# Heads grouped by their place in the pair, and three small products run on eight or four tiles of the TensorE array

## The chip, the core and the metric

The program runs on one core of a Trainium2 chip. The metric is the device time of one execution in microseconds (us). The kernel before takes 1470.96 us, the median of three runs (1470.56 to 1471.3).

## What is computed

Eight batches (`B`), each of eight heads (`H`), 512 tokens (`S`), 32 states (`Ns`) and 64 elements (`D`): tokens read the states, states read the tokens, and what they read goes through two gated layers.

```python
def _attn_ref(x, state):
    scale = 1.0 / np.sqrt(D)
    scores = scale * np.matmul(x, state.transpose(0, 1, 3, 2))   # tokens x states
    a = softmax(scores)                                          # over the 32 states
    xread = np.matmul(a, state)
    scores2 = scale * np.matmul(state, x.transpose(0, 1, 3, 2))  # states x tokens
    a2 = softmax(scores2)                                        # over the 512 tokens
    sread = np.matmul(a2, x)
    return np.concatenate([xread, sread], axis=2)

x = attn_out  as  (B * (S + Ns)) x 512
x = ((x @ w_a) * (x @ w_b)) @ w_out        # 512 -> 1536 -> 512
h = x @ w_in                               # 512 -> 2048
return (h - np.tanh(h)) @ w_out2           # 2048 -> 512
```

## The kernel before

A block is one batch. Blocks 0 to 7 hold the 512 token rows of a batch; block 8 holds the state rows of all eight. The first layer of a block goes over `f` = 0 to 11, 128 hidden columns at a time. For each `f`, `AB` (L507) makes two products of 512 columns into a PSUM tile `pab` (12 matmuls each), multiplies them, and splits the result into a high and a low part (`ph`); `X1` (L533) multiplies that with the output weights into four accumulators `acc` (12 matmuls). The second layer (L679, and all from L897 on) follows when the first is through, and the change does not touch it.

**What is small.** The tokens' read is never formed: `xread @ w` is `a @ (state @ w)`, and `M` (L431) makes `state @ w` for one `f`, a tile `mx` of 128 rows (heads' states) by 512 columns. Blocks 0 and 1 take `mx` from `M` itself; for blocks 2 to 7 `M_later` (L470, tiles `mq` and `mst`) makes it during blocks 1 and 4, writes it to a DRAM tensor `md`, and `M_load` (L495) brings it back. The softmax work of the next block (class `Att`, L272) is spread over the twelve `f` of the block that runs (`stages`, L394): `scores` (`sc`), `scale`, softmax over states (`rows_max`, `rows_norm`, result `hl`) and over tokens (`cols_exp`, `cols_norm`), four transposes (`turn`, tile `pt`), and `sread` (`pr`), the states' read of the tokens.

**How the heads lie.** Two heads that are neighbours form a pair `p` (0 to 3): their elements fill the 128 partitions of `xT`, and their states stand beside each other in `stp`, whose 64 columns for a pair have zeros where a state would meet the other head. A group `G` before is two pairs, so `sc` is 128 rows: a matmul contracts over all 128 partitions and writes 64 of them. Everything from `scores` to `sevac` runs once for `G` = 0 and, some stages later, once for `G` = 1. These products have F32 operands, and each of their matmuls stands as two records in the trace; `AB` and `X1` have one record per matmul.

**What sets the order.** Each engine runs its instructions in the order that a scheduler gave them when the program was built. PSUM has eight banks: four are `acc`, two are `pab`, and all else of the first layer (`sc`, `pt`, `pr`, `mp`, `mq`, `pl`, `pa`) takes turns in two, `p0` and `p1` (`att`, L78). In block 0, `M` holds its bank through a round trip: ScalarE copies the high part out (L442), TensorE subtracts it (L443, weight `minus`), ScalarE copies the rest (L444). In block 1 the rest is VectorE's (L125). VectorE also decodes the weights, above all in block 0 (`words`, L117).

Of the kernel before, what the change touches and what calls it, by code (L numbers as in the profile page):

```python
# [8 lines left out]
F32 = mybir.dt.float32  # L9
# [7 lines left out]
KT = 4  # L17
# [27 lines left out]
def fused_kernel(ctx: ExitStack, tc, xT, xn, stp, stq, wA, wB, outT, outS):  # L45
# [23 lines left out]
    md = [[tc.dram_tile([nb, 2, 2, NST, 2, 256], F32, name=f"md{i}_{f}") for f in range(FA)]  # L69
# [202 lines left out]
    class Att:  # L272
# [12 lines left out]
        def load_xT(self, G, t=None):  # L285
            t = t or big.get([128, 2, 512], F32, "xTt", XIN)
            nc.sync.dma_start(t, xT[self.b, 2 * G : 2 * G + 2].rearrange("q p t -> p q t"))
            self.xT[G] = t

        def load_xn(self, G, t=None):  # L290
            t = t or big.get([128, 4, 256], F32, "xnt", XIN)
            nc.sync.dma_start(t, xn[self.b, :, 256 * G : 256 * G + 256].rearrange("(t p) c -> p t c", p=128))
            self.xn[G] = t

        def scores(self, G):
            ps = self.ps[G] = att.get([128, 512], F32, "sc")
            for q in range(2):
                p = 2 * G + q
                nc.tensor.matmul(ps[64 * q : 64 * q + 64, :], self.stp[:, 64 * p : 64 * p + 64],  # L299
                                 self.xT[G][:, q, :], start=True, stop=True)  # L300

        def scale(self, G, S=None):
            self.S[G] = S if S is not None else small.get([128, 512], F32, "S", AT)
            self.sm[G] = sp.tile([128, 36], F32, tag="sm", name="sm", bufs=2)
            nc.scalar.mul(self.S[G], self.ps[G], 0.125)
# [7 lines left out]
        def rows_max(self, G, L=None):  # L313
            L = self.L[G] = L if L is not None else small.get([128, 512], F32, "L", AT)
# [13 lines left out]
        def rows_norm(self, G):  # L328
# [11 lines left out]
            else:  # L340
                aT = small.get([128, 512], F32, "aT", AT)
                nc.vector.transpose(aT, L)
            hl = HL[self.b][G] = x_tile(2 * (self.b % 2 == 0) + G, [128, 2, 512], "hl")
# [19 lines left out]
        def turned(self, G, t=None):  # L363
            self.E2T[G] = t if t is not None else small.get([128, 4, 128], F32, "E2T", AT)
            nc.scalar.copy(flat(self.E2T[G]), self.pt[G])

        def sread(self, G):
            pr = self.pr[G] = att.get([128, 512], F32, "pr")
            for g in range(2):
                for t in range(4):  # L370
                    for q in range(2):
                        p = 2 * G + q
                        j = 2 * q + g
                        nc.tensor.matmul(pr[32 * p : 32 * p + 32, 64 * g : 64 * g + 64],  # L374
                                         self.E2T[G][:, t, 32 * j : 32 * j + 32],
                                         self.xn[G][:, t, 64 * j : 64 * j + 64],
                                         start=t == 0, stop=t == 3, skip_group_check=True)

        def sevac(self, G):
            if G == 0:  # L380
                self.SR = sp.tile([128, 128], F32, tag="SR", name="SR")
            r = slice(64 * G, 64 * G + 64)
            nc.scalar.copy(self.SR[r, :], self.pr[G][r, :128])
# [10 lines left out]
        def stages(self):  # L394

            none = lambda: None
            yield none, (lambda: (self.scores(0), self.load_xn(0)))
            yield (lambda: (self.scale(0), self.rows_max(0), self.cols_exp(0))), none
            yield (lambda: (self.cols_norm(0), self.rows_norm(0))), (lambda: self.turn(0))
            yield (lambda: self.turned(0)), (lambda: (self.sread(0), self.load_xT(1)))  # L400
            yield (lambda: self.sevac(0)), none
# [584 lines left out]
```

## Time and profile before

| | us |
|---|---|
| median of 3 runs | 1470.96 |
| lowest, highest | 1470.56, 1471.3 |
| the profiled execution's own time | 1472.2 |
| its span in the profile | 1470.4 |

By the page of the profile TensorE's matmuls (PE) are busy for 99% of the span, VectorE (DVE) 77%, ScalarE (ACT) 62%, GpSimd 11%. The chain of work that ended last is PE's for 96%: L424 (`pab` and `acc`) for 66%, and in the small products `mq` 3%, `mp` 2%, `pr` 1%, `sc` 1%. The ends of matmuls are modelled and they overlap, so what a group of them costs is read from the chain, which gives each piece the time until the next begins.

### The profile page before, as it was taken

Reading aid. Unit: us, or ns where it says so; the run is one execution under the profiler, and the core shown is the slowest. Engines: PE = TensorE matmul, PEld = TensorE weight load, DVE = VectorE, ACT = ScalarE, POOL = GpSimd, SP = SyncE. Lnnn points to the kernel's source line nnn. Section 1 sums busy time; section 2 is a strip of 40 time slices with the busy share of each in tenths; the row PEclk is TensorE's granted clock in tenths of the full one; section 3 lists DMA queues with packets and bytes.
Section 4 is the critical chain, followed back from the end, with each engine's and each line's share of the span. In section 5 each row is a group of like instructions: output and inputs, shape, how many; then the busy total and the mean of one; then the engine's idle time right before and its main releaser. Section 6 shows DMA issues by size and latency. Waiting matters only on the chain.

```text
span 1470.4 us, 23250 instructions
## 1 busy us (share of the span) xinstructions
PE 1451.6 (99%) x8660; PEld 1223.9 (83%) x8660; DVE 1128.3 (77%) x1969; ACT 904.4 (62%) x1721; POOL 167.6 (11%) x318
## 2 busy tenths in 40 slices
PE   6999999999999999999999999999999999999999
PEld 3776777777888777888988998998989889889998
DVE  6986546787543778773388899888989898898887
ACT  5764445565443556552367777767777776767675
POOL 0000000222000222220211111111001111111110
PEclk9999999999999999999999999999999999999999
DMA  8733435677455677753966656666675666656544
GB/s 292 242 131 109 153 129 179 216 230 230 123 136 149 188 235 233 237 186 115 314 204 190 207 179 207 194 197 208 187 222 172 209 200 190 209 171 214 169 146 127
DMA packets 102625, 280.44 MB, mean 191 GB/s; under 512 B 14064, under 2 KB 43248, under 8 KB 92784
## 3 DMA queue, kind: packets, MB, share of 16 engines
q0 software_dynamic: 40320, 178.28, 39.8%
q1 hardware_dynamic: 62192, 100.68, 20.7%
q8 instruction: 68, 1.11, 0.3%
q14 instruction: 45, 0.37, 0.1%
HBM read 216.53 MB, written 62.39 MB: 190 GB/s over the span
## 4 chain that ended last, share of the span: by engine, by line
PE 96%; DMA 1%; DVE 1%; ACT 1%; issue 0%; SPq 0%; ACTq 0%; DVEq 0%
PE acc L424 45%; PE pab L424 21%; PE px L609 12%; PE pz L609 6%; PE py L609 3%; PE mq L478 3%; PE mp L437 2%; PE pr L374 1%; PE sc L299 1%; DMA x1d<-ev 1%; DMA rawab<-in_wA 1%; PE pt L310 0%; PE mp L443 0%; PE pa L310 0%; DVE sm L324 0%
## 5 line engine op out<-in xcount | busy, mean ns | idle before, releaser
L424 PE MATMUL acc<-g,wo 128*128 128x512 f32 (+1 forms) x1728 | 436.7, 385 | 0.1
L424 PEld LDWEIGHTS acc<-g,wo 128*128 128x128 f32 x1728 | 293.7, 190 | 40.3 <-DVE g L649 0.3
L424 PE MATMUL acc<-ph,wo 128*128 128x512 f32 (+1 forms) x1296 | 305.1, 383 | 0.5 <-DVE sm L355 0.5
L424 PE MATMUL pab<-hl,mx 128*128 128x512 f32 x1152 | 293.6, 401 | 0.0
L424 PEld LDWEIGHTS acc<-ph,wo 128*128 128x128 f32 x1296 | 231.6, 188 | 52.6 <-issue 3.1
L424 PEld LDWEIGHTS pab<-hl,mx 128*128 128x128 f32 x1152 | 211.6, 189 | 61.8 <-issue 6.7
L524 DVE TENSOR_TENSOR ac<-ac,pab 128x512 f32<-128x512 f32 (+1 forms) x108 | 70.7, 654 | 144.4 <-PE pab L424 143.2
L256 POOL DMA_DIRECT2D wh<-whd x144 | 76.2, 529 | 674.6 <-PE pz L609 607.8
L644 ACT CAST g<-y 128x512 fp32r<-128x512 f32 (+1 forms) x144 | 86.0, 597 | 85.5 <-DVE y L640 84.4
L609 PEld LDWEIGHTS px<-T,wh 128*128 128x128 f32 x768 | 109.5, 190 | 11.0
L609 PE MATMUL px<-B,wh 128*128 128x256 f32 x768 | 113.6, 284 | 2.8 <-ACT snap L715 2.8
L633 DVE SCALAR_TENSOR_TENSOR y<-y,u 128x512 f32<-128x512 f32 (+1 forms) x144 | 95.0, 659 | 26.8 <-ACT y L625 26.1
L609 PEld LDWEIGHTS px<-B,wh 128*128 128x128 f32 x768 | 106.0, 192 | 8.8 <-ACT snap L715 3.3
L609 PE MATMUL pz<-T,wh 128*128 128x256 f32 x768 | 113.1, 283 | 0.0
L609 PE MATMUL px<-T,wh 128*128 128x256 f32 x768 | 112.8, 283 | 0.0
L521 ACT COPY ac<-pab 128x512 f32<-128x512 f32 (+1 forms) x108 | 60.5, 560 | 82.6 <-PE pab L424 82.5
L609 PEld LDWEIGHTS pz<-T,wh 128*128 128x128 f32 x768 | 105.9, 192 | 5.7
L640 DVE COPY_PREDICATED y<-k,t 128x512 f32<-128x512 int32 (+1 forms) x144 | 104.8, 728 | 2.7
L649 DVE TENSOR_TENSOR g<-y,g 128x512 fp32r<-128x512 f32 (+1 forms) x144 | 94.6, 657 | 9.3 <-ACT g L644 9.3
L634 DVE SCALAR_TENSOR_TENSOR u<-t,u 128x512 f32<-128x512 f32 (+1 forms) x144 | 94.3, 655 | 9.0 <-ACT k L629 1.0
L629 ACT ACTIVATE k<-u,consts 128x512 f32<-128x512 f32 (+1 forms) x144 | 99.8, 693 | 0.0
L625 ACT ACTIVATE y<-u,consts 128x512 f32<-128x512 f32 (+1 forms) x144 | 98.8, 686 | 0.7 <-DVE g L649 0.6
(234 smaller groups left out, 2056.8 us busy)
## 6 DMA issues: line engine op xcount, KB each, us to landing
wh<-whd POOLq DMA_DIRECT2D x64, 1024.0 KB, 5.3
wh<-whd POOLq DMA_DIRECT2D x72, 768.0 KB, 4.7
ml<-md POOLq DMA_DIRECT2D x72, 256.0 KB, 3.2
raw<-in_wB SPq DMA_DIRECT2D x32, 512.0 KB, 4.7
whd<-hlb POOLq DMA_DIRECT2D x64, 256.0 KB, 3.8
rawab<-in_wA SPq DMA_DIRECT2D x12, 1024.0 KB, 5.2
md<-mst SPq DMA_DIRECT2D x48, 256.0 KB, 2.6
x1d<-ev SPq DMA_DIRECT2D x32, 256.0 KB, 3.6
```

The lines of the kernel that those rows point to most:

```text
L256: nc.gpsimd.dma_start(t.rearrange("p a h c -> p a (h c)"), whd[j][:, a:b])
L424: nc.tensor.matmul(dst[:, cols], w[a], x[:, c, cols], start=first and i == 0, stop=last and i == 2)
L521: nc.scalar.copy(a[:, :n], pt[:, :n])
L524: at_v = nc.vector.tensor_tensor(a[:, :n], a[:, :n], pt[:, :n], ALU.mult)
L609: nc.tensor.matmul(dst, WP[s, piece][:, a, block(k)], XB[slots[s][0]][x][:, c, k, :], start=first and k == 0 and i == 0, stop=last and k = ...
L625: nc.scalar.activation(y, u, AF.Square, bias=consts[:, 0:1], scale=1.0)
L629: nc.scalar.activation(k, u, AF.Relu, bias=consts[:, 1:2], scale=1.0)
L633: nc.vector.scalar_tensor_tensor(y, y, PK, u, ALU.add, ALU.mult)
L634: nc.vector.scalar_tensor_tensor(u, t, C3, u, ALU.mult, ALU.mult)
L640: nc.vector.copy_predicated(y, k.bitcast(I32), t)
L644: nc.scalar.copy(GG[s, g][:, 0, : width(s)], EW[s, g][2])
L649: nc.vector.tensor_tensor(gt[:, 1, :n], EW.pop((s, g))[2], gt[:, 0, :n].bitcast(F32), ALU.subtract)
```

## The change

A group `G` is now the place in the pair: `G` = 0 has the first heads of all four pairs, `G` = 1 the second. A head's product contracts over its own 64 partitions alone and writes its own 32, so eight matmuls stand in for four, on eight tiles of the array (two by rows, four by columns). The two row halves write two PSUM tiles, in the two banks.

- `scores()` makes both groups at once; it needs both halves of `xT`, which are loaded together.
- `M` writes two tiles of 256 columns; each has its own copies and, in block 0, its own `minus` matmul.
- `sread()` makes both groups in one go, four column tiles of 32 rows at a time, with the same 32 matmuls in all as two visits had before. `sevac` is one copy in place of two.
- The second half of `xT` and of `xn` lies in a buffer that is later the block's `hl` of group 1.
- `md` has another layout, and `M_load` two transfers of 64 partitions for one of 128.
- `stages` has a new order; `rows_norm(1)` comes last.

```diff
+        def load_x(self, src, name, shape, places):
+            halves = []
+            for h in range(2):
+                t = places[h] if places else (big.get(shape, F32, name, XIN) if h == 0
+                                              else xp.tile(shape, F32, tag=f"x{self.hl(1)}", name=name))
+                nc.sync.dma_start(t, src(h))
+                halves.append(t)
+            return halves
-        def scores(self, G):
-            ps = self.ps[G] = att.get([128, 512], F32, "sc")
-            for q in range(2):
-                p = 2 * G + q
-                nc.tensor.matmul(ps[64 * q : 64 * q + 64, :], self.stp[:, 64 * p : 64 * p + 64],
-                                 self.xT[G][:, q, :], start=True, stop=True)
+        def scores(self):
+            for G in range(2):
+                self.ps[G] = att.get([128, 512], F32, "sc")
+            for p in range(KT):
+                for G in range(2):
+                    r = slice(64 * G, 64 * G + 64)
+                    nc.tensor.matmul(self.ps[G][32 * p : 32 * p + 32, :],
+                                     self.stp[r, 64 * p + 32 * G : 64 * p + 32 * G + 32],
+                                     self.xT[p // 2][r, p % 2, :], start=True, stop=True)
-        def sread(self, G):
-            pr = self.pr[G] = att.get([128, 512], F32, "pr")
-            for g in range(2):
+        def sread(self):
+            pr = self.pr = att.get([128, 512], F32, "pr")
+            for G in range(2):
                 for t in range(4):
-                    for q in range(2):
...
+                    for p in range(KT):
+                        c = 128 * (p % 2) + 64 * G
+                        nc.tensor.matmul(pr[32 * p : 32 * p + 32, 64 * G : 64 * G + 64],
+                                         self.E2T[G][:, t, 32 * p : 32 * p + 32],
+                                         self.xn[p // 2][:, t, c : c + 64],
+                                         start=G == 0 and t == 0, stop=t == 3, skip_group_check=True)
-        def sevac(self, G):
...
-            nc.scalar.copy(self.SR[r, :], self.pr[G][r, :128])
+        def sevac(self):
+            self.SR = sp.tile([128, 128], F32, tag="SR", name="SR")
+            nc.scalar.copy(self.SR, self.pr[:, :128])
...
+            yield none, none
+            yield none, (lambda: (self.scores(), self.load_xn()))
+            yield (lambda: (self.scale(0), self.scale(1), self.rows_max(0), self.cols_exp(0))), none
+            yield (lambda: self.cols_norm(0)), (lambda: self.turn(0))
+            yield (lambda: (self.rows_norm(0), self.turned(0))), none
+            yield (lambda: (self.rows_max(1), self.cols_exp(1))), none
+            yield (lambda: self.cols_norm(1)), (lambda: self.turn(1))
+            yield (lambda: self.turned(1)), (lambda: self.sread())
+            yield (lambda: (self.sevac(), self.rows_norm(1))), (lambda: self.turn_s())
             yield (lambda: self.keep_s()), none
...
     def M(blk, f):
-        mp = att.get([128, 512], F32, "mp")
+        mp = [att.get([128, 512], F32, "mp")[:, 0:256] for _ in range(2)]
+        for p in range(KT):
+            for G in range(2):
+                r = slice(64 * G, 64 * G + 64)
+                nc.tensor.matmul(mp[G][32 * p : 32 * p + 32, :].rearrange("p (s c) -> p s c", s=2),
+                                 STP[blk][r, 64 * p + 32 * G : 64 * p + 32 * G + 32], WA[f][r, :, p, :],
+                                 start=True, stop=True)
+        m = MM[blk, f] = mix.get([128, 2, 512], F32R, "mx", *([] if blk == 0 else [MX]))
         for G in range(2):
...
+            c = slice(256 * G, 256 * G + 256)
+            nc.scalar.mul(m[:, 0, c], mp[G], 2.0 ** -8)
+            if blk == 0:
+                nc.tensor.matmul(mp[G], minus, m[:, 0, c], start=False, stop=True, skip_group_check=True)
+                nc.scalar.mul(m[:, 1, c], mp[G], 2.0 ** -8)
...
     def states_split(i):
-        for p in range(KT if i == 0 else 1):
+        for p in range(KT):
...
     def M_load(blk, f):
-        src = md[i][f].rearrange("b q r s g c -> b (q r s) (g c)")
-        nc.gpsimd.dma_start(t, src[b])
+        src = md[i][f].rearrange("g b q s r c -> g b (q s) (r c)")
+        for G in range(2):
+            nc.gpsimd.dma_start(t[64 * G : 64 * G + 64, :], src[G, b])
...
-    A.load_xT(0, t0)
+    A.load_xT((t0, t1))
     A.load_state()
-    A.load_xT(1, t1)
...
-    A.scores(0)
-    A.scores(1)
+    A.scores()
     A.scale(0, tS[:, 0])
```

**Blocks 2 to 6, on TensorE.** The first `f` of block 2, before (`sc` has half of the next block's scores; it comes again five `f` later):

```order
L299 MATMUL sc<-xTt,stp 64x512 x2
L424 MATMUL pab<-hl,mx 128x512 x12
L424 MATMUL acc<-ph,wo_286 128x512 x12
L424 MATMUL pab<-hl,mx 128x512 x12
L424 MATMUL acc<-ph,wo_349 128x512 x12
L310 MATMUL pt<-ident,S 128x128 x4
L424 MATMUL pab<-hl,mx 128x512 x12
L424 MATMUL acc<-ph,wo_455 128x512 x12
L374 MATMUL pr<-xnt,E2T 32x64 x16
```

and in the changed kernel, from the second `f` of the same block, with the end of the group further on:

```order
L316 MATMUL sc<-xTt,stp 32x512 x8
L439 MATMUL pab<-hl,mx 128x512 x12
L439 MATMUL acc<-ph,wo_366 128x512 x12
L439 MATMUL pab<-hl,mx 128x512 x12
L439 MATMUL acc<-ph,wo_463 128x512 x12
L328 MATMUL pt<-ident,S 128x128 x4
...
L328 MATMUL pt<-ident,S 128x128 x4
L439 MATMUL pab<-hl,mx 128x512 x12
L439 MATMUL acc<-ph,wo_826 128x512 x12
L391 MATMUL pr<-xnt,E2T 32x64 x32
```

Two visits to `sc` and two to `pr` per block have become one each; the two visits to `pt` stay. In blocks 1 to 6 all six visits to `sc` have their eight matmuls together, and all six to `pr` their 32.

**Block 0, on TensorE.** The third `M` of block 0 (`wa_343`) with what stands around it, before:

```order
L310 MATMUL pt<-ident,at__174 128x128 x4
L437 MATMUL mp<-wa_343,stp 64x256 x3
L310 MATMUL pl<-ident,S 128x128 x4
L437 MATMUL mp<-wa_343,stp 64x256
L424 MATMUL acc<-ph,wo_286 128x512 x9
L443 MATMUL mp<-mx,minus 128x512
L424 MATMUL acc<-ph,wo_286 128x512 x3
```

and in the changed kernel (`wa_360` is the same weight):

```order
L328 MATMUL pt<-ident,at__174 128x128 x4
L452 MATMUL mp<-wa_360,stp 32x256 x4
L439 MATMUL acc<-ph,wo_300 128x512
L452 MATMUL mp<-wa_360,stp 32x256 x4
L439 MATMUL acc<-ph,wo_300 128x512 x4
L460 MATMUL mp<-mx,minus 128x256
L439 MATMUL acc<-ph,wo_300 128x512
L460 MATMUL mp<-mx,minus 128x256
L439 MATMUL acc<-ph,wo_300 128x512 x2
```

The eight matmuls of an `M` stand in two lots of four, with other matmuls between them, in 5 of the 12 `M` of block 0 and in 2 of the 12 of block 1; before, that was so once, as shown. The scores for block 1 stand in two lots of four as well.

**The start, on ScalarE.** The first instructions before (`at__174` is the scaled scores, `hab` the first step of decoding a weight) and then in the changed kernel:

```order
L305 ACTIVATE at__174<-sc 128x512
L429 ACTIVATE minus<-ident 128x128
L305 ACTIVATE at__174<-sc 128x512
L115 ACTIVATE hab<-rawab 128x1024
L326 ACTIVATE at__175<-at__175 128x512
```

```order
L444 ACTIVATE minus<-ident 128x128
L116 ACTIVATE hab<-rawab 128x1024
L323 ACTIVATE at__174<-sc 128x512 x2
L116 ACTIVATE hab<-rawab 128x1024
L116 ACTIVATE dh<-raw 128x512
L344 ACTIVATE at__175<-at__175 128x512
```

Both scalings of the scores have moved behind the first `hab`, which waits for its weight's load.

## Rows read from the trace of the kernel before

**Rows 1.** The page: busy us of each engine (share of the span) and its instructions.

```profile
PE 1451.6 (99%) x8660; PEld 1223.9 (83%) x8660; DVE 1128.3 (77%) x1969; ACT 904.4 (62%) x1721; POOL 167.6 (11%) x318
```

**Rows 2.** Busy us by stretch: PE, PEld, DVE, ACT, POOL; then clock, DMA.

```profile
25.00:95.00 70.00, 69.30 (x445) 49.03 (x444) 64.57 (x105) 50.61 (x89) 0.00 (x0) 1.00 0.65 224
...
115.00:238.00 123.00, 122.77 (x772) 88.05 (x771) 70.43 (x107) 58.60 (x101) 3.37 (x6) 1.00 0.44 141
249.00:680.00 431.00, 430.89 (x2209) 343.23 (x2210) 293.00 (x528) 223.75 (x397) 78.80 (x146) 1.00 0.62 191
```

**Rows 3.** The chain that ended last, in block 2: start us, us, what.

```profile
270.27 1.01 PE sc L299 x4
271.28 3.00 PE pab L424 x12
...
277.03 2.80 PE pab L424 x12
...
288.58 1.02 PE pr L374 x32
289.60 2.99 PE pab L424 x12
```

**Rows 4.** Timeline of PE, cut to single visits: start us, us, line, operands, records.

```profile
270.20 0.65 PE L299 MATMUL sc<-xTt,stp 128*64 128x512 f32 x2
...
288.51 0.25 PE L374 MATMUL pr<-xnt,E2T 128*32 128x64 f32 x2
...
288.51 1.09 PE L374 MATMUL pr<-xnt,E2T 128*32 128x64 f32 x32
...
186.02 1.08 PE L437 MATMUL mp<-wa,stp 128*64 128x256 f32 x8
...
189.33 0.50 PE L478 MATMUL mq<-wh,sq 64*128 64x256 f32 x4
```

**Rows 5.** Single records by line: ns min/median/max, first and last start.

```profile
L299 PE MATMUL sc<-xTt,stp x56: 592/592/643, 29.7 to 578.0; 128*64 128x512 f32 x56
...
L374 PE MATMUL pr<-xnt,E2T x448: 219/219/244, 55.4 to 596.7; 128*32 128x64 f32 x150
...
L437 PE MATMUL mp<-wa,stp x192: 379/379/690, 16.2 to 216.6; 128*64 128x256 f32 x192
```

**Rows 6.** Timeline of the start: start us, us, engine, line, what, idle before.

```profile
5.06 1.98 PE L299 MATMUL sc<-xin__170,stp 128*64 128x512 f32 x4 [5.06 <-DMA stp<-in_stp]
...
7.95 1.98 PE L299 MATMUL sc<-xin__171,stp 128*64 128x512 f32 x4 [0.91 <-DMA xin__171<-in_xT]
9.85 1.97 PE L310 MATMUL pl<-ident,at__174 128*128 128x128 f32 x8
9.97 0.60 ACT L305 ACTIVATE at__174<-sc 128x512 f32<-128x512 f32 x1 [2.10 <-PE sc L299]
10.56 1.17 ACT L115 ACTIVATE hab<-rawab 128x1024 f32<-128x1024 f32 x1
...
18.33 0.68 DVE L334 TENSOR_TENSOR at__175<-at__175,sm 128x512 f32<-128x512 f32 x1
```

**Rows 7.** Waits in blocks 0 and 1: us in total, times, longest us.

```profile
PEld mp L443 <- ACT mx L442: 3.0, 4, 1.5
...
PE mp L443 <- ACT mx L442: 1.4, 2, 0.7
...
PEld mp L437 <- ACT mst L483: 3.2, 10, 0.6
```

**Rows 8.** Copies out of PSUM: two by form (mean ns), two in block 1.

```profile
L442 ACT ACTIVATE mx<-mp 128x512 fp32r<-128x512 f32 x12 | 7.1, 595 | 5.5 <-PE mp L437 5.3
...
L706 ACT COPY snap<-px 128x256 f32<-128x256 f32 x3 | 1.1, 373 | 3.4 <-PE px L609 3.4
...
205.53 0.59 ACT L483 COPY mst<-mq 128x512 f32<-128x512 f32 x1 [0.99 <-PE mq L478]
205.59 0.69 DVE L485 COPY mst<-mq 128x512 f32<-128x512 f32 x1 [2.56 <-PE mq L478]
```

More of the change, by code (lines that the diff above doesn't have):

```diff
@@ L67, in fused_kernel @@
     wod = [tc.dram_tile([128, 1024], F32R, name=f"wod_{f}") for f in range(FB)]
-    md = [[tc.dram_tile([nb, 2, 2, NST, 2, 256], F32, name=f"md{i}_{f}") for f in range(FA)]
+    md = [[tc.dram_tile([2, nb, 2, NST, 2, 256], F32, name=f"md{i}_{f}") for f in range(FA)]
           for i, nb in enumerate((4, 2))]
@@ L302, in scale @@
+        def scores(self):
[7 more added lines that the diff above has]
+                                     self.xT[p // 2][r, p % 2, :], start=True, stop=True)
         def scale(self, G, S=None):
-            self.S[G] = S if S is not None else small.get([128, 512], F32, "S", AT)
+            self.S[G] = S if S is not None else small.get([128, 512], F32, "S", AT[G : G + 1])
@@ L313, in rows_max @@
         def rows_max(self, G, L=None):
-            L = self.L[G] = L if L is not None else small.get([128, 512], F32, "L", AT)
+            L = self.L[G] = L if L is not None else small.get([128, 512], F32, "L", (AT[2:3], AT[0:1])[G])
             sm, L3 = self.sm[G], L.rearrange("p (k s) -> p k s", s=32)
@@ L340, in rows_norm @@
             else:
-                aT = small.get([128, 512], F32, "aT", AT)
+                aT = small.get([128, 512], F32, "aT", (AT[0:1], AT[2:3])[G])
                 nc.vector.transpose(aT, L)
-            hl = HL[self.b][G] = x_tile(2 * (self.b % 2 == 0) + G, [128, 2, 512], "hl")
+            hl = HL[self.b][G] = x_tile(self.hl(G), [128, 2, 512], "hl")
             nc.scalar.copy(hl[:, 0, :], aT)
@@ L363, in turned @@
         def turned(self, G, t=None):
-            self.E2T[G] = t if t is not None else small.get([128, 4, 128], F32, "E2T", AT)
+            self.E2T[G] = t if t is not None else small.get([128, 4, 128], F32, "E2T", (AT[2:3], AT[1:2])[G])
             nc.scalar.copy(flat(self.E2T[G]), self.pt[G])
-        def sread(self, G):
-            pr = self.pr[G] = att.get([128, 512], F32, "pr")
-            for g in range(2):
+        def sread(self):
+            pr = self.pr = att.get([128, 512], F32, "pr")
+            for G in range(2):
                 for t in range(4):
-                    for q in range(2):
[L372 to L377, printed above, removed]
-        def sevac(self, G):
-            if G == 0:
-                self.SR = sp.tile([128, 128], F32, tag="SR", name="SR")
-            r = slice(64 * G, 64 * G + 64)
-            nc.scalar.copy(self.SR[r, :], self.pr[G][r, :128])
+                    for p in range(KT):
[7 more added lines that the diff above has]
+            nc.scalar.copy(self.SR, self.pr[:, :128])
         def turn_s(self):
@@ L786, in fused_kernel @@
     DO.load()
[L787 to L788 removed]
+    A.load_xn([t.rearrange("p a (b c) -> p (a b) c", c=256) for t in (t2, t3)])
     DO.load()
[L790 to L791 removed]
+    A.scores()
     A.scale(0, tS[:, 0])
```

66 lines of the change are left out of this document (25 added, 41 removed).

## The prediction, made before the changed kernel ran

> **What bounds the kernel now.** I read the page's engine line first, to see which engine has no room: PE is busy 1451.6 of 1470.4 us, and DVE, the next, 77% [rows 1]. An average over stages can mislead, so the second view is busy time by stretch. From 249 to 680 us (blocks 2 to 7) PE is busy 430.89 of 431 us and DVE 293: there every microsecond taken from PE comes off the end. From 115 to 238 us (block 1) it is 122.77 of 123, and DVE has much room. From 25 to 95 us (block 0) PE is busy 69.30 of 70, but DVE 64.57: PE can give back at most about 5.4 us there before DVE, which decodes the weights, sets the pace [rows 2]. Third, the chain of waits in block 2, because its pieces abut: it gives what a visit to a small product costs, its own time and what it does to its neighbour. A visit to `sc` takes 1.01 us, one to `pr` 1.02, and the `pab` behind each takes 3.00 or 2.99 in place of 2.80: 0.20 us to get out of the small tiles [rows 3]. So a visit costs 1.21 or 1.22.
>
> **Do tiles run at the same time?** The sum rests on this. The first two `sc` records are 643 ns long at most and together take 0.65 us; the first two of `pr`, 244 ns at most, together 0.25 [rows 4, 5]: two column tiles start about 6 ns apart and stream side by side. A `pr` visit has 32 records in 16 such pairs, so a pair has (1.09 - 0.22) / 15 = 0.058 us; an `mp` visit has 8 in 4 pairs, (1.08 - 0.38) / 3 = 0.23 us each [rows 4, 5]. Two row tiles also overlap: four `mq` records of 64 rows take 0.50 us [rows 4]. Four column tiles, or rows and columns together, no row shows. The bounds for them are as fast as a pair (a step of 4 or 8 tiles takes what a step of 2 does) and no faster than pairs (twice as many steps). I take the first, since nothing in the pairs' rows gives way: the second tile delays the first by nothing that can be seen.
>
> **Blocks 1 to 6 (attention for blocks 2 to 7).** Scores: two visits of 1.21 become one. It has 16 records on 8 tiles, again two steps, plus six more starts of 6 ns: 1.01 + 0.04 + 0.20 = 1.25. Saved: 2.42 - 1.25 = 1.17. States' read: two visits of 1.22 become one with 64 records on 4 tiles, 16 steps as one visit has now: 1.02 + 0.01 + 0.20 = 1.23, saved 1.21. Together 2.38 a block, six blocks: **14.3 us**. The loads cost nothing: both halves of `xn` are asked for right behind the scores and wanted six `f` later, and the second half of `xT` waits for the last `pab` of the block before, with five groups of twelve L424 matmuls, 2.80 us each [rows 3], between that and the scores. The second `md` load of each `M_load` is on POOL, which is 11% busy [rows 1]. If the cover of `xT` were gone, PE would stand at `sc` for the rest of the load, six times.
>
> **`M` in block 1.** A whole `M` has 16 records on 8 tiles: two steps for four, 2 x 0.23 - 0.04 = 0.42 saved. One in two lots has four tiles per lot, so two steps in each, and enters and leaves twice: 2 x (2 x 0.23 + 0.15 + 0.20) = 1.62 against 1.28 now, 0.34 lost (0.15 is 1.08 less four steps). Ten whole and two in lots: 4.2 - 0.7 = 3.5. Against it stands a wait: `mp` now needs both banks. Behind `mq` PE waits 3.2 us in ten places for ScalarE's copy [rows 7]; VectorE's copy of the other bank starts 0.06 later and takes 0.69 for 0.59, so it ends 0.16 later [rows 8]. Ten times 0.17: 1.7 lost. Queued behind the waiting `mp` on PE are the rest of `pab` and then everything. Left: **1.8 us**, bounds -1 (0.3 more in each) and 3.5 (no wait).
>
> **Block 0.** Seven `M` whole, five in lots: 2.9 - 1.7 = 1.2. The states' reads for blocks 0 and 1: 2 x 1.2 = 2.4. The scores for block 1 stand in two lots and save nothing. Round trips: now PE waits 3.0 + 1.4 us for L442's copy before `minus` [rows 7]. The one copy of 595 ns becomes two of about 373 (nearest row, a 128x256 copy [rows 8]), so the second `minus` is ready 0.15 later; and there are two `minus`, and two last copies of 0.37 for one of 0.60 before either bank is free. I take 0.2 for each of 12: 2.4 lost; bounds 0 (other matmuls stand between) and 0.7 each, 8.4 (a whole second copy of 0.37 and about as much again in handing over).
>
> **The start.** The first scores were ready with the first half of `xT` and the states, and scaled while the second half came; the transposes `pl` began at 9.85 [rows 6]. Now no group is complete before both halves are in, and both scalings stand behind `hab`, which runs 10.56 to 11.73: the first scaled scores come at 12.3, `pl` at 12.4, 2.5 late. VectorE fills some of it with decoding that it had to do anyway, but the softmax that the first `pab` waits for ends with L334, which is behind the same decoding. I take 2.3 lost; bounds 0.5 (all filled) and 3.5 (one more 1.2 us decoding step ahead of it). Block 0 in sum: 1.2 + 2.4 - 2.4 - 2.3 = **-1.1**, bounds -9 and +4 (under the 5.4 of VectorE's room).
>
> **The sum.** 14.3 + 1.8 - 1.1 = 15.0 us off the profiled execution's 1472.2 us, 1457.2. That execution stands 1.2 above the median, so for a median: **1456**. The small edits (one `sevac` for two, a states' split in four pieces, `md`'s layout) are on ScalarE, VectorE and the queues of stretches with room.
>
> **Rivals.**
>
> *No more than two column streams (slower).* Each column tile reads its own moving data from all partitions of its rows; if the array is fed two such streams and no more, four tiles go at the pace of two pairs. What decides is the step of four: from about twice 0.058 us in `pr` on, the gain is gone. Then scores take four steps, 1.01 + 0.86 + 0.20 = 2.1 for 2.42 (two steps more, of (1.01 - 0.15) / 2 each), the read 1.02 + 16 x 0.058 + 0.20 = 2.2 for 2.44: 0.55 a block, 3.3 in six. A whole `M` saves nothing. Block 1: -0.7 - 1.7 = -2.4. Block 0: 0.5 - 1.7 - 2.4 - 2.3 = -5.9. Sum -5.0: 1476. For it: no row shows more than two. Against it: two do not slow each other at all. The Trainium skill ("TensorE: Matmul & The Clock Gate", Measured speedup vs the span model) reports 16 tiles at 10.6 times the pace of one; no run here shows that, nor with F32 operands.
>
> *Starts, not columns, set the pace of the read.* 32 records in 1.02 us is 0.032 us a record. If that is a limit per record, 64 take 2.04 + 0.20 for 2.44, and eight reads lose 1.0 each of what I counted: 1464. Against it: two records that start 6 ns apart [rows 4]. The Trainium skill ("TensorEngine Tiling (Array Packing)", Instruction Overhead) speaks against this part of the change: some 60 cycles for every matmul however few its columns, and no tiling of a product that is small already. As an estimate from that page, 64 records at 60 cycles of 2.4 GHz are 1.6 us, and the time would be 1461; the 6 ns already contradict it if it is meant for tiles side by side.
>
> *The two banks.* 24 `M` now take both `p0` and `p1`, through a round trip, while scores, transposes and reads want them too. At the bad ends of blocks 0 and 1 (-9, -1) the sum is 4.3: 1467; if each `M` cost 0.6 more than I counted, 14 us, it is all gone: 1470. For it: block 0 is where both engines are full, and the two lots show that the banks are short. Against it: in all of blocks 0 and 1 `mp` waits little now [rows 7].
>
> **How the numbers follow.** Forecast (1450 to 1463): 0.66. Starts: 0.10. Banks: 0.10, half of it within 0.2%. Two streams: 0.11. Better than 1450, if block 0 gains all that VectorE allows: 0.03. The bounds of the forecast's own costs give 14.3 + 3.5 + 4 = 21.8, 1449, and 14.3 - 1 - 9 = 4.3, 1467. The range 1449 to 1470 leaves out the two streams and little else. Faster than 1468 (0.2%, 2.9 us, about what a measurement of this kernel can tell): 0.66 + 0.10 + 0.05 + 0.03, less a little for a mistake that I do not see, 0.80; within 0.2%: 0.08; slower: 0.12.
>
> **What would show it.** In blocks 2 to 6 the chain should have one `sc` piece of 16 records near 1.05 us and one `pr` piece of 64 near 1.03, and the distance from one block to the next should be 2.4 us less; a `pr` piece of 2 us is the starts, both near 2 the two streams. A whole `mp` in block 1 should have 16 records in 0.65 us. PE's waits before `mp` and `minus` should total 6 to 12 us in blocks 0 and 1; 20 or more are the banks. The first `pab` should begin about 2.3 us later than now. The forecast fails if a step of four column tiles is not as short as one of two, or if block 0 ends more than 9 us later than it does.

## The result, and the profile after

The changed kernel takes **1453.3 us** (median; 1451.56 to 1453.75), beside 1470.8 for the kernel before on the same chip: a ratio of 0.9882, 95% interval 0.9869 to 0.9895. The forecast was 1456 with 1449 to 1470. The profiled execution of the changed kernel took 1451.56 us, with a span of 1449.8, that is 20.6 less than the span of before; the medians are 17.4 apart. The profiled execution is the fastest of the four, and part of the difference between these two numbers is found below, between the two layers.

The page's engine line for the changed kernel, which answers [rows 1], and the busy time by stretch, which answers [rows 2] (PE, PEld, DVE, ACT, POOL, then granted clock, DMA share, GB/s; the last stretch is again blocks 2 to 7):

```profile
PE 1427.9 (98%) x8928; PEld 1207.5 (83%) x8928; DVE 1129.5 (78%) x1984; ACT 904.8 (62%) x1752; POOL 207.9 (14%) x390
...
25.00:95.00 70.00, 67.43 (x527) 45.16 (x526) 65.30 (x106) 50.90 (x102) 0.00 (x0) 1.00 0.64 225
115.00:238.00 123.00, 123.00 (x892) 87.45 (x891) 74.35 (x125) 61.38 (x114) 6.35 (x12) 1.00 0.49 158
249.00:660.00 411.00, 411.00 (x2204) 331.77 (x2203) 287.57 (x518) 216.83 (x387) 113.08 (x209) 1.00 0.64 196
```

PE still bounds the kernel from block 1 on. In block 0 it does not any more: PE is idle 2.57 of the 70 us, where it was idle 0.70.

The chain of waits in block 2 of the changed kernel, which answers [rows 3] (start us, us, what):

```profile
239.13 1.02 PE sc L316 x16
240.15 3.00 PE pab L439 x12
...
274.59 1.03 PE pr L391 x64
275.62 2.99 PE pab L439 x12
```

One `sc` visit of 16 records and one `pr` visit of 64 stand where there were two of each, and each is as long as one of the two was. The `pab` behind each still takes 0.20 us more than 2.80.

The timeline of PE, cut to the first records of a visit and to whole visits, answers [rows 4] (start us, us, line, operands, records), and the last two rows give single records, as [rows 5] did (ns min/median/max):

```profile
274.52 0.26 PE L391 MATMUL pr<-xnt,E2T 128*32 128x64 f32 x4
...
239.06 0.66 PE L316 MATMUL sc<-xTt,stp 64*32 64x512 f32 x8
...
112.83 0.66 PE L452 MATMUL mp<-wa,stp 64*32 64x256 f32 x16
...
32.84 0.64 PE L452 MATMUL mp<-wa,stp 64*32 64x256 f32 x8
...
36.93 1.06 PE L316 MATMUL sc<-xTt,stp 64*32 64x512 f32 x8
...
L391 PE MATMUL pr<-xnt,E2T x448: 219/219/243, 85.8 to 573.4; 128*32 128x64 f32 x150
...
L316 PE MATMUL sc<-xTt,stp x112: 589/601/613, 36.9 to 537.5; 64*32 64x512 f32 x112
```

Four `pr` records of 243 ns take 0.26 us together and eight `sc` records of 613 ns take 0.66: a tile starts (0.66 - 0.613) / 7 = 7 ns behind the one before it, and all eight stream side by side. A whole `M` of 16 records takes 0.66 us; a lot of 8, which uses the tiles of one row half only, takes 0.64. The fifth row is a score product of block 0, in two lots of 8: each lot takes 1.06 us, which is what 16 take in block 2.

Where the time went is read off the start of the first `pab` of each block on PE's timeline (each block has 144 `pab` records). Lengths of the blocks in us:

| block | before | after | difference |
|---|---|---|---|
| start to the first `pab` | 21.15 | 21.28 | +0.13 |
| 0 | 95.66 | 95.71 | +0.05 |
| 1 | 114.84 | 109.64 | -5.20 |
| 2 | 74.83 | 71.42 | -3.41 |
| 3 | 72.65 | 70.28 | -2.37 |
| 4 | 88.54 | 86.48 | -2.06 |
| 5 | 73.45 | 70.92 | -2.53 |
| 6 | 72.65 | 70.28 | -2.37 |
| 7 | 66.96 | 66.96 | 0 |
| rest (block 8, second layer) | 789.71 | 786.80 | -2.91 |

### The profile page after: what moved, and what is told of

It reads as the page before. It is cut to its first block, busy times and chain, and to the rows that moved or that the text cites. A ratio compares the mean times of both kernels' runs of the same rounds, so it can differ in the third digit from the quotient of the medians.

```text
span 1449.8 us, 23949 instructions
## 1 busy us (share of the span) xinstructions
PE 1427.9 (98%) x8928; PEld 1207.5 (83%) x8928; DVE 1129.5 (78%) x1984; ACT 904.8 (62%) x1752; POOL 207.9 (14%) x390
## 4 chain that ended last, share of the span: by engine, by line
PE 95%; DMA 2%; ACT 2%; DVE 1%; issue 0%; SPq 0%; ACTq 0%; DVEq 0%
PE acc L439 45%; PE pab L439 20%; PE px L630 13%; PE pz L630 6%; PE py L630 3%; PE mq L498 3%; DMA rawab<-in_wA 2%; PE mp L452 1%; PE pr L391 1%; PE sc L316 0%; PE pt L328 0%; ACT hab L116 0%; DMA x1d<-ev 0%; PE mp L460 0%; PE pa L328 0%
## 5 line engine op out<-in xcount | busy, mean ns | idle before, releaser
L520 POOL DMA_DIRECT2D ml<-md x144 | 75.6, 526 | 421.5 <-DVE mx L526 247.5
```

Source lines behind the costliest of these rows:

```text
L520: nc.gpsimd.dma_start(t[64 * G : 64 * G + 64, :], src[G, b])
```

## The experiments

The medians below stand each beside runs of the kernel before on the same chip, as a ratio to it; the changed kernel's own ratio is 0.9882. Four runs undo parts of the change, three lighten one engine's work in block 0, and the rest ask about block 0, the start and the two layers.

**Read in pairs of column tiles.** The order of the records in the states' read is turned so that two column tiles stream at a time, not four:

```diff
-            for G in range(2):
-                for t in range(4):
-                    for p in range(KT):
+            for half, G, t in ((h, G, t) for h in range(2) for G in range(2) for t in range(4)):
+                    for p in (2 * half, 2 * half + 1):
```

> The states' read of the tokens issues its 32 matmuls for column tiles 0 and 1 first and then for tiles 2 and 3, so that two tiles run at a time and not four; all else as in the changed kernel. Theory (four column tiles stream side by side, a step takes what a step of two takes): each of the six pr visits in blocks 1 to 6 grows from 1.03 to 1.03 + 16 x 0.056 = 1.92 us, 5.3 us in all, and the two in block 0 add 0 to 1.8: 1458 to 1461 us. Rival (the gain is only that visits and their exits are fewer): no change, 1453.

Measured 1457.06 us, ratio 0.9916 (0.9901 to 0.9931). The chain in its block 2:

```profile
275.88 1.72 PE pr L390 x64
```

So the same 64 records take 1.72 us by twos and 1.03 by fours. A block is 0.65 longer (70.93 for 70.28), six blocks 3.9. The time is somewhat below the range that was expected; the step of a pair in this long visit is (1.79 - 0.22) / 31 = 0.051 us (1.79 is the visit on the timeline), not 0.058. Four column streams at full pace are real: they are 0.65 us a block of what the read gained, and the rest of its gain is that one visit stands for two.

**`M` without row tiles** (it contracts over 128 rows, with zeros in the other head's half of the states' weights, as before):

```diff
-                                 STP[blk][r, 64 * p + 32 * G : 64 * p + 32 * G + 32], WA[f][r, :, p, :],
+                                 STP[blk][:, 64 * p + 32 * G : 64 * p + 32 * G + 32], WA[f][:, :, p, :],
```

> M contracts over all 128 partitions (the zeros of the other head included) as before the change, so that it has four column tiles and no row tiles; order of instructions as in the changed kernel. Theory (rows and columns of tiles work together): a whole M has four steps in place of two, 0.59 to 1.02 us, ten times in block 1: 4.3 us; M in two lots has four tiles per lot either way and loses nothing; block 0 adds 0 to 3. 1457 to 1461 us. Rival (row tiles give nothing): 1453.

Measured 1458.82 us, ratio 0.9925 (0.9911 to 0.994). Whole visits of `M` on its timeline, and the wait before `mp` over blocks 0 and 1 (which reads the same in the changed kernel):

```profile
115.29 1.09 PE L452 MATMUL mp<-wa,stp 128*32 128x256 f32 x16
...
PEld mp L452 <- ACT mst L503: 2.7, 8, 0.4
```

A whole `M` costs 1.09 in place of 0.66; block 1 is 2.98 longer (112.62), block 0 2.39 (98.10). So row tiles of `M` are worth 3.0 in block 1, less than the 4.3 expected there, and in block 0, which in sum gained nothing, they are worth something too: without them the change would have lost there.

**Scores without row tiles:**

```diff
-                                     self.stp[r, 64 * p + 32 * G : 64 * p + 32 * G + 32],
-                                     self.xT[p // 2][r, p % 2, :], start=True, stop=True)
+                                     self.stp[:, 64 * p + 32 * G : 64 * p + 32 * G + 32],
+                                     self.xT[p // 2][:, p % 2, :], start=True, stop=True)
```

> The same for the scores: contraction over 128 partitions with the zeros, four column tiles, no row tiles. Theory: a visit grows from 1.02 to 1.02 + 2 x 0.44 = 1.9 us, six times: 5.2 us, block 0 nothing (its scores stand in two lots): 1458 to 1459 us. Rival (row tiles give nothing): 1453.

Measured 1457.8 us, ratio 0.9918 (0.9902 to 0.9935). In block 2:

```profile
239.46 1.87 PE sc L316 x16
```

1.87 in place of 1.02, and 0.91 us more in block 3 (71.19 for 70.28), as the theory had it; the time is just under its range.

**All three undone**, so that only the grouping of the heads is left (with its loads, two banks for `M` and two `minus`).

> All three at once: heads grouped by place, one visit each, but the read in pairs of column tiles and scores and M without row tiles. Theory: the parts add up, 14.5 to 19 us: 1468 to 1472, about the kernel before, so the grouping alone gives next to nothing. Rival (fewer visits and exits carry the gain): at least half of the gain stays, 1462 or less.

Measured 1470.49 us, ratio 1.0003 (0.9994 to 1.0013). Grouping alone is worth nothing: blocks 3 to 6 gain 0.5 to 0.9 each, since four visits a block have become two, and the start and block 0 lose it again (first `pab` at 24.23, block 0 98.30). By their ratios the three single undoings cost 5.0, 6.3 and 5.3 us, 16.6 together, and all at once 17.8, each known to some 2 to 3 us. On the timelines, which vary less, blocks 1 to 6 together are 4.4, 3.0 and 5.4 longer, 12.8 in sum, and 12.6 with all three undone: there the parts add up, and grouping alone is worth 5.4. Part of the loss at the start is not the grouping's: in this run the first weight tile began to be scaled at 11.1 us, in the changed kernel at 9.02.

**Is block 0 held by VectorE?** In block 0 VectorE decodes `wA`. One bitwise step, 1.2 us for each of 12 tiles, is left out (the words then have no sign), in the kernel before and in the changed one:

```diff
-            words(t, h_ab.pop(f), raw_ab.pop(f))
+            h_, raw_ = h_ab.pop(f), raw_ab.pop(f)
+            nc.vector.tensor_scalar(t, raw_[:, :, 0], 29, None, ALU.logical_shift_right)
+            nc.vector.scalar_tensor_tensor(t, h_, 3, t, ALU.logical_shift_left, ALU.bitwise_or)
```

> The kernel before, with the last step of the words of wA left out (the bitwise step that copies the sign bit; some 1.2 us of VectorE for each of the 12 output tiles of block 0, 14.6 us in all); the words therefore have no sign and the output differs. It goes with e6_a_light, the same edit in the changed kernel. Theory: in block 0 the kernel before keeps TensorE busy for 69.3 of 70 us (25 to 95), so a lighter VectorE gives it 0 to 1.5 us, all in block 0: 1469 to 1471. Rival (block 0 of both kernels is set by VectorE's words): 3 us or more, below 1468.

Measured 1471.07 us, ratio 1.0015 (1.0006 to 1.0023).

> The changed kernel with the same step of the words of wA left out (output differs). In it TensorE stands idle for 2.6 of 70 us between 25 and 95, and the chain goes through the words and the weights' DMA. Theory: what the eight and four tiles save in block 0 is lost to the decode of wA, which is late next; with 14.6 us less of VectorE there block 0 falls by 1.5 to 2.5 us under its 95.7, and the time to 1450.5 to 1452, so the distance between the light pair is 18 to 20 us where it was 17.4. Rival: block 0's gain is lost at the product of states and weights itself (two banks, lots, round trips to ScalarE), which this edit does not touch: block 0 stays within 0.7 us of 95.7, the time at 1452.5 to 1454, and the distance at 17 or less.

Measured 1454.18 us, ratio 0.9894 (0.9878 to 0.9909). Busy time from 0 to 119 us, summed (PE, PEld, DVE, ACT, POOL): first the changed kernel, then the same with the lighter words.

```profile
sum 119.00, PE 102.13 PEld 68.01 DVE 94.28 ACT 73.70 POOL 0.70; mean PE 34.04 PEld 22.67 DVE 31.43 ACT 24.57 POOL 0.23
...
sum 119.00, PE 104.45 PEld 67.71 DVE 81.43 ACT 71.85 POOL 0.69; mean PE 34.82 PEld 22.57 DVE 27.14 ACT 23.95 POOL 0.23
```

VectorE has 12.9 us less to do, and block 0 is not shorter but 1.2 longer (96.93; in the kernel before 1.7 longer, 97.34; the order of instructions moved with the edit). My theory, that less work for VectorE makes block 0 shorter, falls. But PE has 2.3 us more to do in the second row: its idle time between 25 and 95 us is 0.77 in place of 2.57, and in block 0 `mp` takes more. Since the order moved, the pair does not show that the words hold nothing up. The rival's time held within 0.2 us and its distance too (16.9 between the light pair); its bound for block 0 (95.7 within 0.7) did not.

**The order of the first loads**, in the changed kernel, as it was before: the states between the two halves of the tokens.

```diff
-    A.load_xT((t0, t1))
+    nc.sync.dma_start(t0, xT[0, 0:2].rearrange("q p t -> p q t"))
 ...
+    nc.sync.dma_start(t1, xT[0, 2:4].rearrange("q p t -> p q t"))
+    A.xT = [t0, t1]
```

> The changed kernel, with the first loads in the order of the kernel before (the first half of the tokens, the states, the second half) where the change puts the states behind both halves. The prediction charged the start 2.3 us; the profile shows the first product of a weight tile at 21.28 beside 21.15. Theory: the start is set by wA's words and not by the scores, so the order of the loads is worth 0 to 0.5 us: 1452.5 to 1454, first pab at 21 to 21.6. Rival (the start's term holds and was hidden in that one run by a weight load that landed 1.5 us earlier): first pab 1 to 2.3 us earlier, the time at 1451 to 1452.3.

Measured 1454.03 us, ratio 0.9897 (0.9883 to 0.991). The start of this kernel, then of the changed one, on the timeline (start us, us, engine, line, what, idle before), which answers [rows 6]:

```profile
5.08 1.93 PE L316 MATMUL sc<-xin__170,stp 64*32 64x512 f32 x8 [5.08 <-DMA stp<-in_stp]
...
10.66 1.94 PE L328 MATMUL pl<-ident,at__174 128*128 128x128 f32 x8 [0.79 <-ACT at__174 L323]
10.89 1.14 ACT L116 ACTIVATE hab<-rawab 128x1024 f32<-128x1024 f32 x1
```

```profile
6.21 1.08 PE L316 MATMUL sc<-xin__170,stp 64*32 64x512 f32 x4 [6.21 <-DMA stp<-in_stp]
...
9.02 1.15 ACT L116 ACTIVATE hab<-rawab 128x1024 f32<-128x1024 f32 x1 [6.68 <-DMA rawab<-in_wA]
...
10.80 1.94 PE L328 MATMUL pl<-ident,at__174 128*128 128x128 f32 x8 [2.64 <-ACT at__174 L323]
```

The order of the loads trades one for the other: the states come 1.1 us earlier, `wA`'s first `hab` starts 1.9 later (0.5 of it is its place behind the scalings, since VectorE takes the same tile up at 10.44), and `pl` (0.14 earlier) and the first `pab` (21.61, 0.33 later) stay nearly where they were. The time and the first `pab` are at the upper edge of the theory's ranges; the earlier first `pab` of the rival did not come. The new order brings `wA` forward: with it the first `hab` began at 9.0 to 9.7 us in eight of ten profiles, with the old one at 10.0 to 10.9 in all four. The other two are that of grouping alone, at 11.1, and that of the pieces kept together, at 13.0, where VectorE took the tile up at 9.33 and ScalarE scaled the scores first.

**The kernel before, once more.**

> The kernel before once more, unchanged, for a second profile of it. Two readings rest on one profile: that the first weight tile of wA landed at 10.56 there and at 9.02 in the changed kernel, and that TensorE stood idle and its granted clock fell between the two layers (758 to 762) in before alone. Theory: both vary from run to run, the landing by 1 us or more and the rest after block 8 by 1 to 3 us around 787 to 790. Rival: both return within 0.3 us, and then they belong to the two programs. The time: 1470 to 1471.

Measured 1470.31 us, ratio 1.0001 (0.9992 to 1.001). `hab` began at 10.0, the first `pab` at 20.52. Between the two profiles of before the start of `hab` differs by 0.5 and the rest after block 8 by 0.4 us: less than my theory had, and nearer the rival. Between the two layers PE waits for sums that go out to memory (`x1d`) and back. The chain there, in this run, then in the changed kernel (start us, us, what):

```profile
740.13 5.08 DMA x1d<-ev
...
745.99 1.32 PE px L609 x6
```

```profile
723.41 4.03 DMA x1d<-ev
...
728.22 0.98 PE px L630 x6
```

The granted clock (the third number from the end) behind this wait (at 747 to 751 us, not at 758 to 762 as I wrote above), in the kernel before, in its second run, and in the changed kernel:

```profile
748.00:750.00 2.00, 2.00 (x9) 1.81 (x8) 1.57 (x3) 1.27 (x3) 0.00 (x0) 0.50 0.50 171
```

```profile
746.00:748.00 2.00, 2.00 (x9) 1.81 (x10) 1.39 (x4) 1.60 (x4) 0.00 (x0) 0.60 0.85 312
```

```profile
729.00:731.00 2.00, 2.00 (x14) 1.78 (x13) 1.76 (x3) 1.94 (x5) 0.00 (x0) 1.00 1.01 349
```

PE was idle 2.85, 2.46 and 1.39 us before its first `px`. In the first two the clock fell to its lower level (0.50 of 2.4 GHz) behind it, and the six `px` took 1.65 and 1.32 us for 0.98. The rest after block 8 is 789.7 and 789.3 us in the two profiles of before and 790.2 with its lighter words. Among the programs with grouped heads it goes from 786.7 to 789.4: the changed kernel with lighter words has 789.35 (idle 2.55, the clock fell), with scores undone 789.06 (2.12, it fell), and with `M` undone 787.79 (2.40, it did not fall). So some 1 to 3 us there vary from profile to profile among the programs with grouped heads; that all three of before are at the upper end is not explained by any instruction of the change, and stays open.

**`hab` on GpSimd**, to lighten ScalarE in block 0:

```diff
-            scaled(h_ab[f], raw_ab[f])
+            nc.gpsimd.tensor_scalar(h_ab[f].bitcast(F32), raw_ab[f][:, :, 1].bitcast(F32), 2.0 ** -111, None, ALU.mult)
```

> The changed kernel, with the scaling of wA's second word (hab, 1.16 us of ScalarE for each of the 12 output tiles of block 0) done by GpSimd, which works on nothing else there. In block 0 of the changed kernel TensorE stands idle 2.57 us before products that wait for ScalarE (minus for mx 0.87, acc for ph 1.17), and ScalarE had those copies queued behind a hab that waited for its load. Theory: block 0's gain is lost in these round trips to ScalarE; with 14 us less of ScalarE block 0 falls from 95.7 to 93 to 95, and the time to 1450.5 to 1453. Rival (block 0 is held by the wA loads and words as such, whoever scales them; GpSimd may take longer than 1.16 us for it, which no row shows): block 0 stays at 95.5 or gets up to 4 us longer, the time 1453 to 1458.

Measured 1458.73 us, ratio 0.9931 (0.9918 to 0.9943). One step there (ns min/median/max, first and last start):

```profile
L166 POOL TENSOR_SCALAR hab<-rawab x12: 2802/3293/5576, 9.2 to 91.4; 128x1024 f32<-128x1024 f32 x12
```

The time is above both ranges. The first `pab` comes at 25.46, 4.2 later, and that is most of the loss. Block 0 itself is 95.29, 0.4 shorter, below what I expected from 14 us less on ScalarE, and not even that is a gain: both visits of `pa` (transposes) stand before the first `pab` here, where the changed kernel has one of them behind it. A step that takes three times as long is late in its own way, so the run speaks only weakly against ScalarE.

**All `M` and scores kept whole**, each inside one critical section of the scheduler:

```diff
+        with tc.tile_critical():
             for p in range(KT):
                 for G in range(2):
```

> The changed kernel, with each product of states and weights and each score product kept together in the instruction order, so that all 24 products M of blocks 0 and 1 run as one piece of 16 records on eight tiles; in the changed kernel 16 are whole (0.59 us each) and the others run as two pieces of 8 on four tiles (0.57 us each, as long as a whole one). Theory: 7 to 8 x 0.55 = 4 us less of TensorE, of which the second bank, which is free only after the first group's last copy, takes back about half as waits (and the markers that keep them together some tenths each): 1450 to 1453. Rival: the waits for the bank take all of it or more, 1453 to 1457.

Measured 1556.29 us, ratio 1.0591 (1.0577 to 1.0604): neither theory. The longest wait between 21 and 118 us, and one place of it on PE and on ScalarE:

```profile
ACT mx L460 <- PEq L450: 20.9, 8, 6.7
...
59.03 1.30 PE L454 MATMUL mp<-wa,stp 64*32 64x256 f32 x16 [5.10 <-DVE wa L120]
...
60.54 0.66 ACT L460 ACTIVATE mx<-mp 128x256 fp32r<-128x256 f32 x2 [6.67 <-PEq L450]
```

PE stood 5.10 us for the words of this `M`, and ScalarE, whose next instruction was the copy of it, 6.67 us for the end of the section. In these places the section stood where its data were not ready; block 0 took 119.48 and block 1 159.24. Part of that is the clock: between 25 and 117 us it was granted at 0.91 in the mean and between 117 and 310 at 0.89, where the changed kernel has 1.00. The run shows the price of the section, not of the lots, and what all 24 `M` in one piece would be worth stays unmeasured.

**`acc` of the previous tile behind `M`** in block 0:

```diff
-                nc.tensor.matmul(mp[G][32 * p : 32 * p + 32, :].rearrange("p (s c) -> p s c", s=2),
+                MLAST[0] = nc.tensor.matmul(mp[G][32 * p : 32 * p + 32, :].rearrange("p (s c) -> p s c", s=2),
 ...
-            if f > 0:
+            if f > 0 and blk == 0:
+                with tc.issue_after(MLAST[0].ins):
+                    X1(blk, f - 1)
+            elif f > 0:
```

> The changed kernel, with the output products (acc) of block 0 for the previous output tile queued behind the states-times-weights product of the next, so that fewer of those products are cut in two by them (17 to 19 of 24 whole). Theory: 2 x 0.55 = 1.1 us less in block 0, less what acc no longer covers of ScalarE's copies (0 to 2): block 0 at 94.5 to 96.5, the time 1452 to 1454.5. Rival: acc is the cover of the round trips, and without it block 0 grows by 2 us or more, the time above 1455.

Measured 1456.52 us, ratio 0.9912 (0.9899 to 0.9925). PE's wait for the copies before `minus` in block 0, here and then in the changed kernel (us in total, times, longest), which answers [rows 7]:

```profile
PE mp L462 <- ACT mx L460: 5.0, 6, 1.4
```

```profile
PE mp L460 <- ACT mx L458: 1.6, 3, 0.9
```

The wait grows by 3.4 us and block 0 by 3.3 (99.00), as the rival had it. One such place on PE's timeline here:

```profile
69.85 0.64 PE L454 MATMUL mp<-wa,stp 64*32 64x256 f32 x8
71.61 0.39 PE L462 MATMUL mp<-mx,minus 128*128 128x256 f32 x1 [1.13 <-ACT mx L460]
```

Nothing stands between a lot of `M` and its `minus`, and PE waits 1.13 us for ScalarE's copy. Where `acc` or `pab` stand there, as in most places of the changed kernel, they hide it; taken away, they are missing about one for one.

**Half of the round trips.** The second group's remainder in block 0 is taken by VectorE, as in block 1:

```diff
-            if blk == 0:
+            if blk == 0 and G == 0:
```

> The changed kernel, where in block 0 the second group's remainder (m minus its rounded part) is taken by VectorE from the bank, as in block 1 (0.417 us each), and only the first group's by the minus product and a second ScalarE copy (0.385 us). 12 products of minus (0.16 us each, more where they wait) and 12 ScalarE copies go, 12 VectorE steps (5.0 us) come; the round trips in which TensorE waits for ScalarE are halved. Theory: these round trips are what held block 0 at 95.7; it falls by 2 to 3.5 us and the time to 1450 to 1451.8, and VectorE has room for 5 us (taking 14.6 us from it made nothing faster). Rival (VectorE, busy for 65.3 of 70 us, is at its cap): block 0 stays or grows by up to 4 us, the time 1453 to 1457.

Measured 1455.07 us, ratio 0.9891 (0.9874 to 0.9908), no better than the changed kernel. Block 0 falls by 1.2 to 94.53, but the first `pab` comes 1.4 later (22.70), and block 1 begins at 117.23 for 116.99. The 1.2 is no gain: both visits of `pa` stand before the first `pab` here, and PE has 1.1 us less of transposes in block 0. So the theory's 2 to 3.5 do not come. The time is in the rival's range, but its reason does not hold: VectorE is busy 63.44 of 70 us between 25 and 95, where it was 65.30. No version beat the changed kernel.

## Why the prediction was right, and where it was off

**Tiles side by side: right.** Everything rested on four and eight tiles streaming as two do, which no row of before showed. The forecast had `sc` at 1.05, `pr` at 1.03 and a whole `M` at 0.65; they take 1.02, 1.03 and 0.66 (timeline). The rival of two column streams wanted 2 us in both `sc` and `pr`, that of starts 2 us in `pr`; both fall. The estimate from the Trainium skill's "TensorEngine Tiling (Array Packing)", Instruction Overhead, does not hold for tiles side by side: 64 records in 1.03 us are 16 ns each, where its 60 cycles would be 25. The advice in the same section is put more narrowly than the prediction puts it: it warns against taking the tiling factor from a dimension that is already small.

**Attention, 14.3 us for six blocks: right.** Blocks 3 to 6 are 2.37, 2.06, 2.53 and 2.37 shorter, mean 2.33 for the 2.38 of the sum. Two single undoings put a price on its tiles: 0.65 a block for the read and 0.91 for the scores. The other 0.8 or so is the fewer visits, which grouping alone shows (72.65 to 71.88 in block 3).

**`M` in block 1, 1.8 us: too small.** Block 1 is 5.20 shorter, 2.87 more than attention explains. PE's time in `mp` there falls from 10.30 to 7.75 us and in `mq` by 1.0; `pab` and `acc` take 0.6 more. The step that failed is the wait for the second bank, counted at 1.7. PE does not wait there: in the 123 us of this stretch it was idle 0.23 [rows 2] and is idle 0.00 now. The row that the wait was built on [rows 7] is not PE's but that of the weight loads (PEld), which overlap PE: 3.2 us in ten places before, 2.7 in eight now, about 0.3 each, and before `mq` the loads stood as long, 8.2 us in 23 places, where the profile shows nothing that they waited for. Grouping alone has the second bank and no row tiles; its block 1 is 0.62 shorter than before and its blocks 3 to 6 are 0.75 shorter in the mean, so the bank costs about 0.1. The bound "3.5 (no wait)" was nearer the 2.87 than 1.8, and the 2.98 of undoing the row tiles agrees with the measured 2.87.

**Block 2: a term that I did not have.** It is 3.41 shorter, 1.08 beyond the mean of blocks 3 to 6. PE was idle 0.49 us of it before, in `acc`, for VectorE, and not at all after; the rest lies in `pab` and `acc`. With all three parts undone block 2 is 73.06, already 1.77 shorter than before, 1.0 beyond the 0.75 of blocks 3 to 6 in that run. So the term belongs to the grouping with its new order of stages and its buffers, and not to the tiles; which of these edits brings it was not tested.

**Block 0 and the start, -1.1: near, with parts that moved.** Block 1's first `pab` comes 0.19 us later than before. Summing PE's records between the first `pab` of block 0 and that of block 1:

| us of PE in block 0 | before | after |
|---|---|---|
| `mp` (`M` and `minus`) | 16.50 | 14.41 |
| `pr`, `pf` (read) | 4.71 | 2.50 |
| `sc` | 1.87 | 1.99 |
| `pa`, `pl`, `pt` (transposes) | 3.65 | 4.73 |
| `pab`, `acc` | 68.24 | 69.52 |
| idle | 0.70 | 2.57 |
| sum (to rounding) | 95.66 | 95.71 |

The products give back 4.3 us, a little more than the 1.2 and 2.4 of the sum (whose first term leaves out the `minus`). Against it stand 1.9 us more idle, 1.3 in stretched `pab` and `acc`, and 1.1 of transposes, most of it one visit of four that ran ahead of the first `pab` before. The "2.4 for round trips" has about the right size, idle and stretched together being 3.1, but its ground was misread: the 3.0 and 1.4 us of [rows 7] are PEld's and PE's waits in the same places, counted twice, and part of the stretch is the second way out of the small tiles (0.20 us [rows 3]) of each `M` in two lots. The bounds that I gave for block 0 with the start, -9 and +4, come to -8.3 and +3.1 from their own terms; the forecast does not rest on them. One such place in the changed kernel, on PE and ScalarE:

```profile
26.29 0.66 PE L452 MATMUL mp<-wa,stp 64*32 64x256 f32 x16
26.42 1.15 ACT L116 ACTIVATE hab<-rawab 128x1024 f32<-128x1024 f32 x1
...
27.46 0.61 ACT L547 CAST ph<-ac 128x512 fp32r<-128x512 f32 x1
...
27.97 0.67 ACT L458 ACTIVATE mx<-mp 128x256 fp32r<-128x256 f32 x2
28.12 0.30 PEld L439 LDWEIGHTS acc<-ph,wo 128*128 128x128 f32 x2 [1.65 <-ACT ph L547]
28.13 0.50 PE L439 MATMUL acc<-ph,wo 128*128 128x512 f32 x1 [1.17 <-ACT ph L547]
```

`M` is done at 26.95, but ScalarE goes through `hab` first, in its own order, then `ph`, then the copies of `M`, and PE stands 1.17 us for `ph`. That the waits for ScalarE cost PE time, and that `acc` is their cover, is shown (3.4 us of wait, 3.3 of block). That they hold all of block 0's lost gain is not: with half of the round trips gone, block 1 began no earlier. VectorE's words as the holder are made unlikely, since with 12.9 us less of them block 1 began no earlier either (117.70 for 116.99), but not excluded, because the order moved with that edit. What sets block 0's length in the end stays open.

**The start, 2.3: too large.** In the one pair of profiles it is 0.13, with one visit of `pa` moved behind the first `pab`, but that pair is not typical: the first `pab` begins at 20.50 to 21.15 in three profiles of programs with the heads as before, and at 20.77 to 22.70, median 21.73, in seven of programs with the changed start (those with a late `wA` and the run on GpSimd aside). So some 1.0 us seems to be lost, with a spread as large between the profiles. The step that was mis-sized is the place of the scaled scores: I put them behind a `hab` at 10.56, as in the profile of before; the new order of loads brings `wA` 1 to 1.5 us earlier, and `hab` has had its turn when the scores are scaled at 10.08.

**The sum.** 15.0 us were forecast and 17.4 measured between the medians. In the two profiles the terms are 14.0 (2.33 x 6), 2.87, 1.08, -0.19 and 2.91 for the rest, 20.7 in sum; the last of these varies from run to run and was in no term.

## What to carry to other kernels

Where a small product enters and leaves a tiled part of the array, count its visits and its steps, not its records: eight tiles of F32 operands stream in the time of one, so a product that fills only one row half pays the whole price (0.64 us for 8 records, 0.66 for 16). Regrouping the work so that such tiles can be filled may cost as much as it gives by itself (here 1.0003), and must be counted together with the tiles that it allows. In a stretch where several engines are nearly full, take a saving on one as an upper bound, and look in the order of the other engine (here ScalarE's) for what stands ahead of the step that is waited for.

## What the runs showed of the hardware

Eight F32 tiles side by side, four columns by two rows, hardly slow each other: a record of `sc` takes 601 ns in the median in a step of eight and took 592 in a step of two [rows 5]. GpSimd needs 2.8 to 5.6 us for a 128x1024 scaling that ScalarE does in 1.16. The same write of sums to memory between the layers lay on the chain for 4.03 to 5.47 us in three profiles, and where PE had stood idle for it, its clock was at its lower level behind it in some runs and not in others, at nearly the same idle time (it fell behind 2.12 us with the scores undone and not behind 2.40 with `M` undone).
